# Crossbar transposes for half of the q and k of a sliding-window attention with an MLP behind it

## The chip, the cores and the metric

One core of a Trainium2 chip. The metric is device time in microseconds (us), median of several executions; lower is better. Names used below: TensorE (matmuls and their weight loads, PE and PEld in the profile), VectorE (DVE), ScalarE (ACT), GpSimd (POOL), SyncE (SP, which here issues nearly all DMAs). SBUF and PSUM are the two memories that these kernels use: their tiles lie in SBUF, TensorE's results in PSUM. A "hole" is a stretch in which TensorE is idle. Ratios are always the mean time of one kernel's fast runs over the mean of the other's fast runs of the same rounds, so they are not quite the ratio of the medians quoted. A run counts as slow when it is over 1.5% above the fastest run of the same kernel.

## The reference

Attention with a causal window of 64 over 8 batches, 8 heads, 576 tokens, head dimension 64; then, per token, a normalisation and a two-layer MLP of 512 to 2048 to 512 with ReLU, added to the attention's output.

```python
scores = scale * np.matmul(q, k.transpose(0, 1, 3, 2))
mask = (rel >= 0) & (rel < 64)             # rel = query position - key position
attn = softmax(np.where(mask, scores, -1e9))
x = np.matmul(attn, v)                      # heads side by side: (8, 576, 512)
xn = (x - mean) / np.sqrt(var + 1e-6) * g_ln
out = x + np.maximum(xn @ w_ch1, 0.0) @ w_ch2
```

## The kernel before

The kernel works in nine groups. Group g runs the MLP of batch g on the first 512 tokens; group 8 runs it for the last 64 tokens of all batches, which were collected as four "tails" of two batches each. From group 2 on, the MLP of group g is cut into 30 units (16 of the first layer, 14 of the second, which is done with seven products instead of eight). Work for other batches is placed between the units, at numbered slots: the attention of batch g+1, and the loads, casts and transposes of batch g+2. So a slot is a place in the program order of every engine.

The kernel transposes q and k for the scores, so that the head dimension lies on the partitions. Before, TensorE does it, 128x128 at a time, and ScalarE moves the result out of PSUM:

```python
def t_main(b, x, half, eng=None):               # x: 0 for q, 1 for k
    tp = t_tile([128, 8, 128], ...)
    for i in range(8):
        nc.tensor.transpose(out=tp[:, i, :], in_=src[:, i], identity=ident16)
    ...
    evac(x if eng is None else eng, dst..., tp...)

def cast_tail(i):                               # GpSimd, in this order
    vt = p_va.tile([128, 2, H, D + 1], FP16, tag="vt", bufs=1)
    nc.gpsimd.memset(vt[:, :, :, D:D + 1], 1.0)
    nc.gpsimd.tensor_copy(out=q16, in_=tq)
    nc.gpsimd.tensor_copy(out=k16, in_=tk)
    nc.gpsimd.tensor_copy(out=vt[:, :, :, 0:D], in_=tv)

# the schedule of groups 2 to 7; n = g + 2
at(11, cast_qk, n, 0)
at(16, cast_qk, n, 1)
for i, (x, half) in zip((17, 19, 21, 25), ((0, 0), (1, 0), (0, 1), (1, 1))):
    at(i, t_main, n, x, half, 0)
at(27, s_mm, n, 0)                              # first scores of batch n
at(17, load_qk, n + 1, 0)                       # 1 MB each
at(18, load_qk, n + 1, 1)
at(23, load_v, n + 1, 0, 4)
# tails: loads at slot 5, cast at 24, transposes at 27 and 29, scores at slot 1 of the next group
# stores of the group's own rows stand in units 27 and 29
```

The softmax here doesn't subtract the row's maximum and nothing guards it: scores larger than these inputs give would overflow.

## Time and profile before

| | before |
|---|---|
| median of 2 runs | 324.47 us (324.37 to 324.57) |
| span in the profile | 322.6 us |
| TensorE busy | 309.6 us, 96% |
| mean granted clock | 0.996 |
| idle TensorE up to its last matmul, summed from the matmul records | 7.6 us, of it 1.4 us after 90 us |

The first lines are from the page of the kernel before: the busy row of TensorE, the clock granted to TensorE in 40 slices (tenths of full speed), and the main DMA queue (packets, MB, share of 16 engines' time).

```profile
PE 309.6 (96%) x3229; PEld 204.6 (63%) x3229; DVE 204.3 (63%) x388; ACT 176.8 (55%) x292; POOL 164.6 (51%) x251
...
PEclk9999999999999999999999999999999999999998
...
q1 hardware_dynamic: 84816, 48.11, 55.6%
```

The next lines are from the chain of waits of the kernel before (start, length, what), in the second half of group 3. They follow each other without a hole: TensorE is always the one waited for. The pieces "tp x8" are eight transposes of q or k, 0.45 us together, 56 ns each (the first piece of a group, shown here, stands in the chain with 0.55 us). (The group table gives 225 ns for one; as eight take 0.45 us together, they overlap.)

```profile
149.72 1.75 PE pA L435 x16
151.47 0.38 PE xps L291 x16
151.85 0.55 PE tp L216 x8
152.40 0.87 PE pB L435 x8
...
162.92 0.34 PE sc L263 x16
163.26 1.85 PE pC L435 x16
```

And SyncE's own timeline of the kernel before for the same group (start, time at the instruction, operation). The loads of the next batch's first half are at 147.8 us, those of the second half at 153 us. v follows at 158.8 and the stores at 163.7 us.

```profile
147.81 0.39 SPq L92 DMA_DIRECT2D qk<-in_q_dram  x1
148.80 0.39 SPq L92 DMA_DIRECT2D qk<-in_k_dram  x1
152.95 0.37 SPq L92 DMA_DIRECT2D qk<-in_q_dram  x1
153.94 0.37 SPq L92 DMA_DIRECT2D qk<-in_k_dram  x1
158.82 4.68 SPq L139 DMA_DIRECT2D v<-in_v_dram  x4
163.68 4.14 SPq L401 DMA_DIRECT2D out_dram<-xn  x4
```

### The profile page before, as it was taken

To read this page: it belongs to the slowest core of one execution; us is meant where nothing else is said; L and a number is where in the kernel's file an instruction comes from. 1 tells how busy PE (TensorE), PEld (TensorE's weight loads), DVE (VectorE), ACT (ScalarE), POOL (GpSimd) and SP (SyncE) were. 2 spreads that over 40 slices of the span, in tenths; PEclk is the share of its full clock that TensorE was granted. 3 is DMA by queue.
4 is the path that set the end of the run, shared out by engine and by line. 5 is a ranking of instruction groups with operands and counts; after the bars stand their busy time and mean duration, and the time that the engine had idled before them with its cause. 6 is when DMAs were issued, how large, how long until landed. Compare 5 with 4: busy or idle time off the path is not lost.

```text
span 322.6 us, 7813 instructions
## 1 busy us (share of the span) xinstructions
PE 309.6 (96%) x3229; PEld 204.6 (63%) x3229; DVE 204.3 (63%) x388; ACT 176.8 (55%) x292; POOL 164.6 (51%) x251
## 2 busy tenths in 40 slices
PE   7978999999989999999999999999999999999993
PEld 4556444687544578656964696459755865694582
DVE  0887764666885795489447954896559644751643
ACT  2576624487346754876457647775486157405600
POOL 7678765423991689079705982598036506200000
PEclk9999999999999999999999999999999999999998
DMA  8999999976089947904598459000570190003013
GB/s 194 282 385 259 363 306 295 264 267 133 35 276 227 207 139 204 241 2 133 173 259 183 132 168 259 26 2 2 171 182 2 24 241 33 0 2 131 0 36 98
DMA packets 85639, 51.08 MB, mean 158 GB/s; under 512 B 55682, under 2 KB 76674, under 8 KB 85603
## 3 DMA queue, kind: packets, MB, share of 16 engines
q1 hardware_dynamic: 84816, 48.11, 55.6%
q0 software_dynamic: 640, 2.33, 3.1%
q8 instruction: 25, 0.41, 0.5%
q10 hardware_dynamic: 146, 0.13, 0.1%
q14 instruction: 12, 0.09, 0.1%
HBM read 38.80 MB, written 9.44 MB: 150 GB/s over the span
## 4 chain that ended last, share of the span: by engine, by line
PE 85%; DVE 4%; SPq 3%; DMA 2%; POOL 2%; ACT 1%; issue 0%; ACTq 0%; POOLq 0%
PE hps L363 33%; PE pA L435 11%; PE pC L435 8%; PE pB L435 8%; PE hph L484 6%; PE ch L375 4%; PE xps L291 4%; PE tp L216 3%; PE sc L263 3%; DMA w1s<-in_moe_w_ch_dram 2%; PE ztp L328 2%; SPq L139 2%; POOL w1g L188 1%; PE ch L499 1%; DVE wT L532 1%; SPq L87 1%
## 5 line engine op out<-in xcount | busy, mean ns | idle before, releaser
L363 PE MATMUL hps<-zT,w1g 128*128 128x512 f16 x480 | 112.0, 379 | 0.0
L367 ACT ACTIVATE hrT<-hps 128x512 f16<-128x512 f32 x120 | 71.9, 599 | 35.1 <-PE hps L363 31.6
L363 PEld LDWEIGHTS <-w1g 128*128 128x128 f16 x480 | 44.1, 98 | 47.0 <-issue 1.0
L316 POOL TENSOR_SCALAR rsz<-mvg 128x1 f32<-128x1 f32 x28 | 12.2, 437 | 76.5 <-DVE mvg L302 75.5
L266 ACT ACTIVATE pt<-sc 128x512 f16<-128x512 f32 x72 | 39.0, 595 | 14.6 <-PE sc L263 13.1
L435 PEld LDWEIGHTS <-sS 128*128 128x128 f16 x448 | 43.0, 98 | 4.7
L207 ACT COPY qkT<-tp 128x1024 f16<-128x1024 f16 x26 | 26.2, 1012 | 33.6 <-PE tp L216 32.4
L126 POOL CAST qk<-qk 128x1024 f16<-128x1024 f32 x32 | 33.7, 1070 | 9.5 <-DMA qk<-in_q_dram 4.9
L442 DVE TENSOR_TENSOR xn<-pA,xn 128x512 f32<-128x512 f32 x28 | 19.2, 686 | 26.1 <-PE pA L435 17.4
L331 ACT COPY zT<-ztp 128x512 f16<-128x512 f16 x36 | 21.1, 586 | 26.5 <-PE ztp L328 26.1
L435 PEld LDWEIGHTS <-hrT 128*128 128x128 f16 x336 | 32.3, 98 | 5.0
L294 DVE RECIPROCAL rcp<-xps 128x8 f32<-128x8 f32 x36 | 7.4, 205 | 34.3 <-PE xps L291 34.1
L414 DVE TENSOR_TENSOR sS<-hrT 128x512 f16<-128x512 f16 (+1 forms) x42 | 21.4, 510 | 10.2 <-ACT hrT L367 10.2
L297 DVE TENSOR_TENSOR xn<-xps,rcp 128x512 f32<-128x512 f32 x36 | 24.9, 692 | 3.3 <-DMA out_dram<-xn 2.2
L435 PE MATMUL pA<-wT,sS 128*128 128x256 f16 x224 | 26.9, 273 | 0.0
L435 PE MATMUL pC<-w2s,sS 128*128 128x256 f16 x224 | 26.8, 273 | 0.0
L273 DVE TENSOR_TENSOR pt<-pt,mask 128x1024 f16<-128x1024 f16 x28 | 21.2, 762 | 8.6 <-ACT pt L266 8.5
L484 PE MATMUL hph<-zT,w1g 128*128 128x256 f16 x192 | 23.6, 273 | 2.5 <-ACT zT L331 1.1
L299 DVE BATCH_NORM_STATS2 stats<-xn 128x6 f32<-128x512 f32 x36 | 25.0, 695 | 1.2
L319 POOL TENSOR_SCALAR z<-xn,rsz 128x512 f16<-128x512 f32 x28 | 23.4, 836 | 2.9
L375 PE MATMUL ch<-w2s,hrT 128*128 128x512 f16 x96 | 23.7, 380 | 0.1
L484 PEld LDWEIGHTS <-w1g 128*128 128x128 f16 x192 | 18.0, 98 | 5.8 <-issue 2.2
(85 smaller groups left out, 437.2 us busy)
## 6 DMA issues: line engine op xcount, KB each, us to landing
out_dram<-xn SPq DMA_DIRECT2D x34, 256.0 KB, 3.6
qk<-in_q_dram SPq DMA_DIRECT2D x16, 512.0 KB, 4.8
qk<-in_k_dram SPq DMA_DIRECT2D x16, 512.0 KB, 5.9
v<-in_v_dram SPq DMA_DIRECT2D x32, 256.0 KB, 6.2
w2s<-in_moe_w_ch_dram SPq DMA_DIRECT2D x12, 512.0 KB, 5.6
w1s<-in_moe_w_ch_dram SPq DMA_DIRECT2D x4, 512.0 KB, 7.3
tk<-in_k_dram SPq DMA_DIRECT2D x8, 256.0 KB, 4.4
tv<-in_v_dram SPq DMA_DIRECT2D x8, 256.0 KB, 5.1
```

The costliest lines, as they stand in the source:

```text
L126: nc.gpsimd.tensor_copy(out=dst[:, :].rearrange("p (a j) e d -> p a e j d", j=j), in_=t[:, :].rearrange("p (a e j d) -> p a e j d", e=2, j ...
L207: nc.scalar.copy(out=out, in_=in_)
L266: nc.scalar.activation(out=pt[:, par], in_=sc[par], func=AF.Exp, bias=0.0, scale=scale)
L297: nc.vector.tensor_tensor(out=xn, in0=xps[:, :, 0:D], in1=rcp_b, op=ALU.mult)
L299: nc.vector.bn_stats(out=stats, in_=xv)
L319: nc.gpsimd.tensor_scalar(out=z, in0=xv, scalar1=rs, scalar2=nm, op0=ALU.mult, op1=ALU.add)
L363: nc.tensor.matmul(out=hps, lhsT=w1g[:, kc, 128 * hc:128 * (hc + 1)], rhs=zT[g][:, kc, :], start=(kc == 0), stop=(kc == NKC - 1),)
L367: nc.scalar.activation(out=hrT[:, hc, :], in_=hps, func=AF.Relu, bias=0.0, scale=1.0)
L375: nc.tensor.matmul(out=ch[kb], lhsT=hrT[:, hc, 128 * kb:128 * (kb + 1)], rhs=w2s[:, hc, :], start=(hc == 0), stop=(hc == NHC - 1),)
L414: nc.vector.tensor_tensor(out=o, in0=x, in1=y, op=op)
L435: nc.tensor.matmul(out=bank[which][:, p, :], lhsT=a[:, c, 128 * p:128 * p + 128], rhs=wv[:, c, :], start=(first and p == 0 and c == 0), st ...
L484: nc.tensor.matmul(out=hps[:, e], lhsT=w1g[:, kc, 128 * hc:128 * (hc + 1)], rhs=zT[g][:, kc, 256 * half:256 * half + 256], start=(kc == 0) ...
```

## The change

Intent: take the transposes of q and k of batches 4 to 7, and of all tails, off TensorE and let the DMA crossbar do them, from SBUF to SBUF. The casts now write to two fixed buffers, of which the tails share k's (not shown in the cut below). The transposed layout differs, so k is loaded in its natural order (runs of 256 bytes), q stays in an order of four interleaved tokens, and the exponential puts it right by its access pattern. v loads move behind the stores; the residual buffers of groups 4 and later swap places, so that the next group's first block takes the one that was stored first.

```diff
+    XQ = 4
+            elif b >= XQ and x == 1:            # load_qk: k in natural order
+                for c in range(2):
+                    nc.sync.dma_start(out=..., in_=src[b, :, s0:s0 + 128, :].rearrange("h s d -> s h d"))
 def t_main(b, x, half, eng=None):
+        if b >= XQ:
+            if half == 0:
+                nc.sync.dma_start_transpose(out=dst..., in_=cast16[x]...)      # 512 KB
+            return
 # t_tail: the same, dma_start_transpose for q and for k of a tail
-            nc.scalar.activation(out=pt[:, par], in_=sc[par], func=AF.Exp, ...)
+            if XQ <= g < NGRP - 1:
+                o = o.rearrange("p h w (r j) -> p (h w) r j", j=4)
+                i = i.rearrange("p h w (j r) -> p (h w) r j", j=4)
+            nc.scalar.activation(out=o, in_=i, func=AF.Exp, ...)
+                for h in ((1, 0) if g // 2 == 2 else (0, 1)):                   # b_step: pairs swap homes
+                    x_norm[(g, h)] = p_xn.tile(...)
-            ts = (10, 11, 14, 20) if n else (1, 2, 5, 11)
+            ts = (10, 11, 15, 20) if n else (5, 6, 10, 15)
-            for i, ... in zip((17, 19, 21, 25), ...
+            for i, ... in zip((17, 17, 17, 17) if n >= XQ else (17, 19, 21, 25), ...
-                at(23, load_v, n + 1, 0, 4)
+                at(31, load_v, n + 1, 0, 4)
-                at(24, cast_tail, i)
-                at(27, t_tail, i, 0)
-                at(29, t_tail, i, 1)
+                at(22, cast_tail, i)
+                at(22, t_tail, i, 0)
+                at(22, t_tail, i, 1)
```

More of the change, by code (lines that the diff above doesn't have):

```diff
@@ L41 @@
     EPS = 1e-6
+    XQ = 4
+    XZ = 99
     scale = 1.0 / (D ** 0.5)
@@ L77 @@
     qk32, qk16, v32 = {}, {}, {}
+    cast16 = [p_const.tile([128, NHP, 4, 128], FP16, tag=f"cast16_{x}", name=f"cast16_{x}") for x in range(2)]
     tail32, tail16, tailT, vT = {}, {}, {}, {}
@@ L90, in load_qk @@
                 )
+            elif b >= XQ and x == 1:
+                for c in range(2):
+                    s0 = 256 * half + 128 * c
+                    nc.sync.dma_start(
+                        out=t[:, 512 * c:512 * c + 512].rearrange("p (h d) -> p h d", h=H),
+                        in_=src[b, :, s0:s0 + 128, :].rearrange("h s d -> s h d"),
+                    )
             else:
@@ L110, in cast_tail @@
         q16 = p_in.tile([128, H, D], FP16, tag="tq16", name=f"tq16_{i}", bufs=1)
-        k16 = p_in.tile([128, 2, H, D], FP16, tag="qk16_1", name=f"tk16_{i}")
+        k16 = cast16[1][:, 0:2].rearrange("p r c (e d) -> p r (c e) d", d=D)
         vt = p_va.tile([128, 2, H, D + 1], FP16, tag="vt", name=f"vt_{i}", bufs=1)
@@ L122, in cast_qk @@
             t = qk32.pop((b, x, half))
-            dst = p_in.tile([128, 8, 2, D], FP16, tag=f"qk16_{x}", name=f"qk16_{x}_{b}_{half}")
+            if b >= XQ and x == 1:
+                nc.gpsimd.tensor_copy(
+                    out=cast16[x][:, :, 2 * half:2 * half + 2, :].rearrange("p a c m -> p c a m"),
+                    in_=t[:, :].rearrange("p (c a m) -> p c a m", c=2, a=NHP),
+                )
+                continue
+            dst = cast16[x][:, 2 * half:2 * half + 2, :, :].rearrange("p a c (e d) -> p (a c) e d", d=D)
             qk16[(b, x, half)] = dst
@@ L202, in alloc_qkT, with flat @@
         qkT[b] = [p_qkt.tile([128, NHP, SM + 64 * x], FP16, tag=f"qkT{x}", name=f"qkT{x}_{b}") for x in range(2)]
-        nc.gpsimd.memset(qkT[b][1][:, :, 0:64], 0.0)
+        if b < XQ:
+            nc.gpsimd.memset(qkT[b][1][:, :, 0:64], 0.0)
+        else:
+            nc.gpsimd.memset(qkT[b][1][:, 0, 0:64], 0.0)
+    def flat(b, x):
+        return qkT[b][x][:, :, :].rearrange("p h m -> p (h m)")
     def evac(x, out, in_):
@@ L211, in t_main @@
     def t_main(b, x, half, eng=None):
+        if b >= XQ:
+            if half == 0:
+                dst = flat(b, x)[:, 64 * x:64 * x + NHP * SM]
+                nc.sync.dma_start_transpose(out=dst.rearrange("p (a t) -> p a t", t=128),
+                                            in_=cast16[x][:, :, :, :].rearrange("p a c m -> p (a c m)"))
+            return
         src = qk16.pop((b, x, half))
@@ L229, in t_tail @@
                         p_qkt.tile([128, 2, NHP, 128], FP16, tag="tkT", name=f"tkT_{i}", bufs=1))
+            if XQ < B:
+                nc.sync.dma_start_transpose(out=tailT[i][0], in_=src[:, :, :].rearrange("p h d -> p (h d)"))
+                return
             tp = t_tile([128, NHP, 128], f"tpq_{i}")
@@ L233, in t_tail @@
         else:
+            if XQ < B:
+                nc.sync.dma_start_transpose(out=tailT[i][1][:, :, :, :].rearrange("p r h t -> p (r h) t"),
+                                            in_=src[:, :, :, :].rearrange("p r h d -> p (r h d)"))
+                return
             tp = t_tile([128, 2, NHP, 128], f"tpk_{i}")
@@ L258, in s_mm @@
                         rhs = tailT[j][0][rows, hp, 64 * iw:64 * iw + 64]
+                    elif g >= XQ:
+                        c0 = SM * hp + 64 * (2 * j + iw)
+                        lhsT = flat(g, 1)[rows, c0:c0 + 128]
+                        qb = flat(g, 0)[rows, SM * hp + 16 * (2 * j + iw):SM * hp + 16 * (2 * j + iw) + 16]
+                        rhs = bass.AP(tensor=qb.tensor, offset=qb.offset, ap=[qb.ap[0], [128, 4], [1, 16]])
                     else:
@@ L265, in s_mm @@
         for par in range(2):
-            nc.scalar.activation(out=pt[:, par], in_=sc[par], func=AF.Exp, bias=0.0, scale=scale)
+            o, i = pt[:, par], sc[par][:, :]
+            if XQ <= g < NGRP - 1:
+                o = o.rearrange("p h w (r j) -> p (h w) r j", j=4)
+                i = i.rearrange("p h w (j r) -> p (h w) r j", j=4)
+            nc.scalar.activation(out=o, in_=i, func=AF.Exp, bias=0.0, scale=scale)
     def s_mask(g, j):
@@ L278, in b_step @@
         if kb % 2 == 0:
-            x_norm[(g, kb // 2)] = p_xn.tile([128, 2, DM], FP32, tag="xn" + sfx, name=f"xn_{g}_{kb // 2}", bufs=nb)
+            if (g, kb // 2) not in x_norm:
+                for h in ((1, 0) if g // 2 == 2 else (0, 1)):
+                    x_norm[(g, h)] = p_xn.tile([128, 2, DM], FP32, tag="xn" + sfx, name=f"xn_{g}_{h}", bufs=nb)
         xv = x_norm[(g, kb // 2)][:, kb % 2, :]
@@ L325, in zt_step @@
             zT[g] = p_grp.tile([128, NKC, 512], FP16, tag="zT" + sfx, name=f"zT_{g}", bufs=1 if sfx else 2)
+        if g >= XZ:
+            nc.sync.dma_start_transpose(out=zT[g][:, :, 128 * kb:128 * kb + 128], in_=z)
+            return
         ztp = t_tile([128, NKC, 128], f"ztp_{g}_{kb}")
@@ L745 @@
             at(21, make_vB, n)
-            for i, (x, half) in zip((17, 19, 21, 25), ((0, 0), (1, 0), (0, 1), (1, 1))):
+            for i, (x, half) in zip((17, 17, 17, 17) if n >= XQ else (17, 19, 21, 25),
+                                    ((0, 0), (1, 0), (0, 1), (1, 1))):
                 at(i, t_main, n, x, half, 0)
```

## The prediction

> **What bounds the kernel now.** TensorE. It is busy for 96% of the 322.6 us span (engine table; granted clock 0.996), and the chain of waits is 85% TensorE. From about 98 us to 317 us that chain is an almost unbroken row of matmul pieces. So in groups 2 to 8 a TensorE instruction removed should shorten the run by its own pace, and a new TensorE wait should lengthen it in full.
>
> **Removed from TensorE.** The instruction order shows 352 fewer load and matmul rows: 176 transposes, 32 in each of batches 4 to 7 (128) and 12 in each of four tails (48). The chain shows eight of them as pieces of 0.45 us (56 ns each; the 225 ns mean of one is latency). 22 pieces x 0.45 = 9.9 us. All lie on the chain. ScalarE also loses 16 evacuations of 1.01 us and eight for tails, off the chain. Without new waits: 324.5 - 9.9 = 314.6 us.
>
> **Added.** Sixteen crossbar transfers on the SyncE queue: per batch q and k, 512 KB each, plus two smaller ones per tail. [...] No trace shows one yet. Batch k loads now come in 256-byte runs, as v does. Exponentials now read PSUM strided; I expect the same 595 ns.
>
> **Main batches.** In the timeline of group 3 the last q/k cast ends at 153.9 us and the first scores of that batch start at 162.85 us. Taking out 1.8 us of transposes leaves about 7.1 us for both transfers. [...] on time, or late by up to 1 or 2 us, four times. Expected cost 1 us in all, with a long tail. v loads now follow the stores, and swapping residual pairs gives a group's first attention block the buffer stored first (2.2 us of VectorE wait before, off the chain).
>
> **A new wait in group 7.** The fourth tail's cast starts with a memset of the single buffered v tile, so GpSimd waits until TensorE has used the third tail's (before: 10.8 us of GpSimd wait, hidden). That use moves from slot 5 to slot 10, and the fourth tail's scores stay in slot 10, directly behind it in TensorE's order. Between them must now fit: memset 0.15, q cast 0.6, k cast 1.0 (durations in the timeline at 268 us), the crossbar transfer of k and its landing [...]. TensorE stops for about 5 us. This gives back half of the gain.
>
> **Prediction.** 314.6 + 5 + 1 = about 320.5 us, range 315 to 327. Faster by over 2%: 0.27; within 2%: 0.65; slower: 0.08.
>
> **What would show it.** TensorE busy falls by about 10 us by pace; groups 3 to 6 last 1.5 to 2 us less each (now 32 to 33.5 us); one TensorE wait of 4 to 6 us at the scores of the fourth tail, on a DMA; at the first scores of batches 4 to 7 waits on the crossbar transfers of 0 to 2 us; exponentials near 595 ns.
>
> **What would make it wrong.** Crossbar transfers much slower (q and k over 8 us together): TensorE waits four times, and the run is slower than before. Much faster ones: the group 7 wait shrinks to 3 us and the change gains over 2%. Scores reading q in 16-element runs being slower.

The sum came to 314.6 + 5 + 1 = 320.6, put as about 320.5 us, with 314.6 = 324.5 - 9.9. The 5 and the 1 are estimates.

## The result, and the profile after

347.75 us, median of 2 runs (347.25 to 348.24); ratio 1.0717, 95% interval 1.065 to 1.0785. The change makes the kernel 7% slower.

The same rows of the page, after:

```profile
PE 310.0 (89%) x3053; PEld 197.6 (57%) x3053; DVE 207.9 (60%) x388; ACT 156.0 (45%) x268; POOL 162.6 (47%) x251
...
PEclk9999999999999999699996999899999999899999
...
q1 hardware_dynamic: 120272, 53.88, 66.1%
```

TensorE is busy for as long as before, although it executes 176 matmuls less (3053 instead of 3229), and the clock row now has four dents. The time between the starts of the groups' first layers says where it was lost:

| group | 2 | 3 | 4 | 5 | 6 | 7 |
|---|---|---|---|---|---|---|
| before, us | 32.8 | 33.3 | 32.8 | 33.3 | 30.6 | 29.2 |
| after, us | 30.9 | 40.0 | 38.0 | 41.1 | 29.9 | 35.3 |

Groups 2 and 6 are faster, as intended. TensorE's matmul records show one long hole in each of the others: 3.3 us at 137 us (before the first tail's scores), 4.3 us at 179 us (before an attention block), 5.2 us at 215 us (before the second tail's scores), 5.4 us at 290 us (before the fourth tail's). The waits view of the kernel after (who waits for whom: us in total, times, longest) names the releasers, first for TensorE, then for VectorE:

```profile
PE sc L303 <- DMA tkT<-cast: 13.9, 3, 5.4
PE xps L337 <- DVE pt L317: 5.0, 2, 4.3
...
PE sc L303 <- DMA qkT<-cast: 0.9, 2, 0.5
```

```profile
DVE xn L343 <- DMA out_dram<-xn: 23.5, 3, 9.4
```

Before, VectorE's line for the same wait was:

```profile
DVE xn L297 <- DMA out_dram<-xn: 2.2, 3, 1.7
```

So stores of the residual buffers free these too late, by up to 9.4 us; VectorE then gives the attention block's masks late (before the hole at 179 us ends, its L343 starts at 180.92 us after 6.59 us of idle, the mask behind it at 182.47 us), and TensorE waits for VectorE ("pt L317"). The transposed q and k of the main batches, by contrast, cost 0.9 us in two waits: they are not the problem. Here is SyncE's timeline after, from the end of group 2 into group 3:

```profile
119.90 5.09 SPq L237 DMA_TRANSPOSE qkT<-cast  x2
125.04 0.59 SPq L102 DMA_DIRECT2D qk<-in_q_dram  x1
125.67 2.34 SPq L97 DMA_DIRECT2D qk<-in_k_dram  x2
128.06 1.54 SPq L102 DMA_DIRECT2D qk<-in_q_dram  x1
129.64 4.39 SPq L97 DMA_DIRECT2D qk<-in_k_dram  x2
134.13 2.74 SPq L259 DMA_TRANSPOSE tqT<-tq  x1
136.96 1.25 SPq L266 DMA_TRANSPOSE tkT<-cast  x1
138.31 2.00 SPq L450 DMA_DIRECT2D out_dram<-xn  x4
```

Two transposes hold the queue for 5.1 us. Then all six loads of the next batch, 2 MB, are issued together, for 9.0 us (DMA share 1.1 from 125 to 134 us, 1.2 to 140 us); before, half of them had gone at slot 17, ahead of this place, because their buffers were free. Only then come the tail's transposes (134 us) and the stores (138 us), one after the other.

What a hole does to the clock is seen in the windows view of the kernel after. Columns: the stretch, its length, busy us (and instructions) of PE, PEld, DVE, ACT, POOL, the granted clock, the DMA share, GB/s. The hole before the first tail's scores ends at 140.1 us; from 141.45 to 148.3 us the clock is halved.

```profile
139.00:141.00 2.00, 0.91 (x19) 0.60 (x20) 0.00 (x0) 0.47 (x1) 0.00 (x0) 1.00 1.07 352
141.00:143.00 2.00, 2.00 (x7) 0.49 (x4) 1.46 (x3) 1.11 (x3) 0.00 (x0) 0.61 0.99 257
143.00:145.00 2.00, 1.32 (x34) 1.10 (x34) 1.81 (x5) 0.63 (x2) 1.61 (x3) 0.50 1.04 234
145.00:147.00 2.00, 2.00 (x9) 0.89 (x8) 1.93 (x5) 1.26 (x3) 1.37 (x3) 0.50 0.90 198
147.00:149.00 2.00, 2.00 (x9) 0.80 (x8) 1.18 (x2) 1.17 (x3) 1.77 (x3) 0.68 0.31 69
```

The trace's clock record has four such stretches, of 6.8, 6.8, 3.4 and 3.4 us; leaving out the parts in which TensorE was idle anyway, about 18.5 us. From one 128x512 matmul of the first layer to the next it is 0.427 us at half clock (145 to 148 us) and 0.216 us at full clock, so half of that time is lost: 9.3 us. In the kernel after, full and half clock take turns from 11.75 us on, for 129.71, 6.83, 34.13, 6.83, 30.72, 3.41, 71.68, 3.41 and 47.79 us, all whole multiples of 3.41 us. When the trace is cut into pieces of that length, from 11.75 us on, the four at whose end the clock fell held 2.05, 3.41, 3.35 and 3.41 us of idle TensorE; none of the others held more than 1.84 us. The first of the four ends at 141.45 us, with 2.05 us of the 3.3 us hole in it. In the kernel before, whose longest hole is 1.4 us, the clock did not fall before the last matmul. What a piece with 1.84 to 2.05 us of idle does, these two traces do not show.

This closes the account of the time: 9.9 us of transposes less, 23.5 us of idle TensorE more (31.0 against 7.6), 9.3 us lost at half clock: +22.9 us, against a measured 346.5 - 322.6 = 23.9 us of span.

Two things that the change could have spoilt, it did not: the exponentials take 595 ns with the reordering pattern as without, and sixteen score matmuls take 0.34 us in the chain as before.

### The profile page after: what moved, and what is told of

The parts are those of the page before. It is cut to its first block, busy times and chain, and to the rows that moved or that the text cites. A ratio compares the mean times of both kernels' runs of the same rounds, so it can differ in the third digit from the quotient of the medians.

```text
span 346.5 us, 7472 instructions
## 1 busy us (share of the span) xinstructions
PE 310.0 (89%) x3053; PEld 197.6 (57%) x3053; DVE 207.9 (60%) x388; ACT 156.0 (45%) x268; POOL 162.6 (47%) x251
## 4 chain that ended last, share of the span: by engine, by line
PE 57%; POOL 10%; SPq 9%; DVE 8%; DMA 7%; ACT 4%; issue 3%; POOLq 0%; DVEq 0%; ACTq 0%
PE hps L412 23%; PE hph L533 6%; PE pA L484 6%; PE pC L484 4%; PE pB L484 4%; SPq L97 3%; PE xps L337 3%; PE ch L424 3%; DMA out_dram<-xn 3%; PE sc L303 2%; SPq L102 2%; DMA vB<-vA 2%; ACT pt L310 2%; DVE stats L345 2%; DVE xn L343 2%
## 5 line engine op out<-in xcount | busy, mean ns | idle before, releaser
L412 PE MATMUL hps<-zT,w1g 128*128 128x512 f16 x480 | 118.0, 397 | 0.0
L412 PEld LDWEIGHTS <-w1g 128*128 128x128 f16 x480 | 46.1, 101 | 53.0 <-issue 8.8
L343 DVE TENSOR_TENSOR xn<-xps,rcp 128x512 f32<-128x512 f32 x36 | 24.9, 691 | 24.6 <-DMA out_dram<-xn 23.5
L491 DVE TENSOR_TENSOR xn<-pA,xn 128x512 f32<-128x512 f32 x28 | 19.2, 685 | 21.6 <-PE pA L484 16.6
L463 DVE TENSOR_TENSOR sS<-hrT 128x512 f16<-128x512 f16 (+1 forms) x42 | 23.8, 566 | 10.1 <-ACT hrT L416 10.1
L317 DVE TENSOR_TENSOR pt<-pt,mask 128x1024 f16<-128x1024 f16 x28 | 21.8, 785 | 12.6 <-ACT pt L310 12.6
L142 POOL CAST cast<-qk 128x1024 f16<-128x1024 f32 x24 | 25.3, 1061 | 8.4 <-DMA qk<-in_q_dram 3.9
L337 PEld LDWEIGHTS <-pt 128*64 128x64 f16 x576 | 12.5, 113 | 19.1 <-issue 8.2
L363 POOL TENSOR_TENSOR rsz<-rsz,mhalf 128x1 f32<-128x1 f32 x28 | 20.2, 721 | 2.3
```

Source lines behind the costliest of these rows:

```text
L142: nc.gpsimd.tensor_copy(out=dst[:, :].rearrange("p (a j) e d -> p a e j d", j=j), in_=t[:, :].rearrange("p (a e j d) -> p a e j d", e=2, j ...
L337: nc.tensor.matmul(out=xps[64 * r:64 * r + 64, h, :D + 1], lhsT=pt[:, par, hp, r, :], rhs=rhs, start=True, stop=True)
L343: nc.vector.tensor_tensor(out=xn, in0=xps[:, :, 0:D], in1=rcp_b, op=ALU.mult)
L412: nc.tensor.matmul(out=hps, lhsT=w1g[:, kc, 128 * hc:128 * (hc + 1)], rhs=zT[g][:, kc, :], start=(kc == 0), stop=(kc == NKC - 1),)
L463: nc.vector.tensor_tensor(out=o, in0=x, in1=y, op=op)
```

## The experiments

Eighteen kernels were run in all, in five sessions, each with its own runs of before. "Idle" is idle TensorE up to its last matmul in the profiled run.

| run | what | median us | ratio to before | 95% interval | idle us |
|---|---|---|---|---|---|
| before | | 324.5 to 325.2 by session | | | 7.6 |
| after | | 347.75 | 1.072 | 1.065 to 1.079 | 31.0 |
| e1 | q and k on the crossbar, tails on TensorE | 337.24 | 1.039 | 1.034 to 1.045 | 21.4 |
| e2 | q and k loads behind the stores | 328.40 | 1.010 | 1.005 to 1.015 | 17.9 |
| e3 | memset of the v tile after the casts | 340.95 | 1.047 | 1.042 to 1.053 | 24.7 |
| e4 | stores issued by GpSimd | 347.19 | 1.069 | 1.063 to 1.076 | 30.6 |
| e5 | k in 1 KB runs (order of keys wrong) | 340.76 | 1.049 | 1.046 to 1.051 | 27.9 |
| e6 | tails alone on the crossbar | 331.53 | 1.020 | 1.018 to 1.023 | 14.5 |
| e7 | first half of q, k loaded early | 333.74 | 1.028 | 1.025 to 1.031 | 22.1 |
| e8 | e2 with idle matmuls in the hole of group 7 | 328.87 | 1.008 | 1.004 to 1.013 | 16.3 (slow run) |
| s1 | v loads and swapped pairs alone | 324.32 | 0.999 | 0.997 to 1.000 | 7.4 |
| b1 | e2 and e3 together | 325.40 | 1.001 | 0.999 to 1.002 | 16.2 |
| b3 | b1, first half loaded early | 327.18 | 1.009 | 1.005 to 1.013 | 15.5 |
| b4 | b1, two steps in later slots | 325.26 | 1.001 | 0.997 to 1.004 | 14.2 |
| f1 | e6 with idle matmuls in the hole of group 7 | 329.62 | 1.015 | 1.012 to 1.018 | 10.1 |
| b5 | b1, tails of groups 3 and 5 moved to group 6 | 327.27 | 1.007 | 1.005 to 1.010 | 17.6 |
| b6 | b5 with later slots | 326.33 | 1.004 | 1.002 to 1.006 | 17.1 |
| b7 | b1 with k in 1 KB runs (order of keys wrong) | 320.81 | 0.987 | 0.984 to 0.989 | 12.5 |
| b9 | b6, tail transposes and loads behind the stores | 325.67 | 1.002 | 1.000 to 1.004 | 16.6 |
| b10 | b9 with only batches 6 and 7 on the crossbar | 331.66 | 1.018 | 1.016 to 1.021 | 19.5 (slow run) |

The first theory was a queue theory: SyncE's order holds tail transposes and stores behind the loads. Its rival was traffic: crossbar reads and short runs fill the DMA engines, whatever the order.

### e1: tails back on TensorE

```diff
-            if XQ < B:                     # t_tail, twice
+            if XT:                         # XT = False
-            ts = (10, 11, 15, 20) if n else (5, 6, 10, 15)
+            ts = (10, 11, 14, 20) if n else (1, 2, 5, 11)
-                at(22, cast_tail, i); at(22, t_tail, i, 0); at(22, t_tail, i, 1)
+                at(24, cast_tail, i); at(27, t_tail, i, 0); at(29, t_tail, i, 1)
```

> The changed kernel with the tails' transposes back on TensorE, in the slots of before; q and k of batches 4 to 7 stay on the crossbar. Queue theory (one in-order SyncE queue holds tail transposes and stores behind six loads; TensorE then idles 3.3, 4.3, 5.2 and 5.4 us and its clock halves after each): the three waits for the tails' transposed k go (13.9 us, and about 7 us of their half clock), 48 transposes come back (2.7 us): about 330 us, and the 4.3 us gap at 179 us, which is a late store, stays. Traffic rival (crossbar reads and 256-byte k loads fill the DMA engines, so every transfer is late whatever the order): the tails' waits go but VectorE waits for stores as long as before (over 20 us), about 337 to 343 us.

337.2 us: between the two. The holes for transposed tails are gone, but others of 3.9, 2.7, 1.8 and 5.3 us stand at the same three group starts (the one of 2.7 us waits for another DMA, a copy of v), and VectorE still waits 14.3 us for stores. The stores are now issued directly behind the six loads (at 133.5, 170.8 and 204.4 us), and still too late. So the tail transposes were not what held the stores. In front of them are left the two transposes and the six loads; e2 tells which. This also prices the main half of the change: q and k alone on the crossbar cost 12 us over the 325.2 us of before.

### e2: q and k loads behind the stores

```diff
-                at(17, load_qk, n + 1, 0)
-                at(18, load_qk, n + 1, 1)
+                at(31, load_qk, n + 1, 0)
+                at(31, load_qk, n + 1, 1)
```

> The changed kernel with the q and k loads of the next batch moved from directly behind the transposes to behind the stores; nothing else. Same bytes, same packets. Queue theory: tail transposes and stores are issued about 9 us earlier, the gaps at 137, 179 and 215 us (3.3, 4.3, 5.2 us) and their half clock go, the one in group 7 stays: 326 to 330 us; the casts of q and k may now wait for their loads by some us. Traffic rival: the traffic is the same, so about 345 to 348 us with the gaps somewhere else.

328.4 us, as the queue theory said: 19 us from two lines, with the same bytes in the same packets. The stretch of SyncE's timeline of e2 that answers to the one shown above:

```profile
120.25 5.04 SPq L237 DMA_TRANSPOSE qkT<-cast  x2
128.25 1.26 SPq L259 DMA_TRANSPOSE tqT<-tq  x1
129.96 1.23 SPq L266 DMA_TRANSPOSE tkT<-cast  x1
131.28 2.00 SPq L450 DMA_DIRECT2D out_dram<-xn  x4
133.34 0.75 SPq L102 DMA_DIRECT2D qk<-in_q_dram  x1
```

The stores are issued at 131.3 instead of 138.3 us, and the three holes at 137, 179 and 215 us are gone; of VectorE's 23.5 us of waits for stores 0.6 us are left. What remains of TensorE's waits is group 7's and small ones:

```profile
DVE xn L343 <- DMA out_dram<-xn: 0.6, 1, 0.6
```

```profile
PE sc L303 <- DMA tkT<-cast: 5.4, 1, 5.4
PE ztp L377 <- POOL z L365: 4.2, 3, 1.4
...
PE sc L303 <- DMA qkT<-cast: 1.9, 3, 0.8
```

### e3: one memset later

```diff
-        nc.gpsimd.memset(vt[:, :, :, D:D + 1], 1.0)
         nc.gpsimd.tensor_copy(out=q16, in_=tq)
         nc.gpsimd.tensor_copy(out=k16, in_=tk)
+        nc.gpsimd.memset(vt[:, :, :, D:D + 1], 1.0)
```

> The changed kernel with one line moved: in the cast of a tail the memset of the v tile comes after the casts of q and k, not before. It tests the wait in group 7 alone: the fourth tail's k is cast and transposed long before its scores. Theory of the prediction: the 5.4 us gap at 290 us and the 3.4 us at half clock behind it go, 347.7 - 5.4 - 1.7 = about 340.6 us, all else as it was. Rival, that the crossbar transfer itself is slow there: the gap stays, 347 us.

340.95 us, 0.3 us from the number expected. First the kernel after, GpSimd's timeline in group 7: the memset waits for TensorE's third tail (14.48 us of idle GpSimd), and the casts come behind it, right when TensorE wants the fourth tail's scores.

```profile
290.30 0.17 POOL L125 MEMSET vt<- 128x16 f16 x1 [14.48 <-PE xps L337]
...
290.98 1.04 POOL L127 CAST cast<-tk 128x1024 f16<-128x1024 f32 x1
```

In e3 both casts run before the memset, which now waits alone, and the hole of 5.4 us is gone:

```profile
280.13 1.04 POOL L126 CAST cast<-tk 128x1024 f16<-128x1024 f32 x1 [0.32 <-DMA tk<-in_k_dram]
286.19 0.17 POOL L127 MEMSET vt<- 128x16 f16 x1 [5.01 <-PE xps L337]
```

### e4: stores on another queue

```diff
-            nc.sync.dma_start(out=out[g, ...], in_=x_norm[...])
+            (nc.gpsimd if g > 1 else nc.sync).dma_start(out=out[g, ...], in_=x_norm[...])
```

> The changed kernel with the stores of groups 2 to 7 issued by GpSimd instead of SyncE. Queue theory: the stores start when VectorE has finished them, VectorE's 23.5 us of waits for stores fall under 5 us, the 4.3 us gap at 179 us goes; the tails' transposes are still behind the loads, so the gaps of 3.3, 5.2 and 5.4 us stay: 337 to 341 us. Traffic rival: stores land as late as before, VectorE's waits stay over 15 us, 345 to 348 us.

347.2 us: no gain, the expectation missed. GpSimd does issue the stores early, at 129.8 and 131.3 us (SyncE: 138.3 us), but they land late: a median of 6.6 us after their issue, against 3.5 us for the stores of the kernel after, and VectorE still waits 14 us for them. The issuing engine alone does not explain this: in e4 the twelve stores beside the bursts of groups 2 to 4 took 6.0 to 8.4 us, the four of group 7, with little else under way, 2.4 to 4.7 us. The lines are from e4's list of DMA issues and from its waits view:

```profile
out_dram<-xn POOLq DMA_DIRECT2D x24, 256.0 KB, 6.6
```

```profile
DVE xn L343 <- DMA out_dram<-xn: 14.0, 4, 4.7
```

So a free queue was not enough here (347.2 us against 347.75). The waits for transposed tails, which still stand behind the loads, even grew from 13.9 to 17.4 us.

Both pure theories had failed: the queue alone (e1, e4) and the traffic alone (e2, where the traffic is the same). What fits all four runs is a burst theory: the 2 MB of loads, issued in one piece behind the transposes, occupy the DMA engines for about 9 us, and whatever is issued after them, on any queue, is late. The order decides what is in front. The next runs test that.

### e5: longer runs for k

```diff
-            elif b >= XQ and x == 1:
+            elif False:                    # k goes the way of q, in 1 KB runs
```

> The changed kernel with k of batches 4 to 7 loaded in runs of 1 KB as before instead of 256 bytes (the order of tokens is then wrong and so is the result, on purpose; the work is the same). Burst theory, as the first four runs left it: 2 MB of q and k loads are queued at once between the transposes and the stores and fill the DMA engines for about 9 us; the size of the runs only changes how long. The loads take 1 to 2 us less per batch, the gaps at 137, 179 and 215 us shrink but stay: 338 to 344 us. Rival, that the 256-byte runs are the cause: those three gaps go, 326 to 330 us.

340.8 us, inside the range of the burst theory: the holes shrink to 1.0 and 1.5, 1.5 and 2.5, and 3.3 us and stay. The keys are then in a wrong order. The comparison with the reference passed it all the same. A likely reason, only argued: q and k are 0.1 times standard normal numbers, the scaled scores then have a spread of about 0.01, and all weights in a window are nearly equal. It is no version to use; it also means that this comparison would hardly notice a permuted k, in any of the kernels.

### e6: tails alone

```diff
-    XQ = 4
+    XQ = 8
-            if XQ < B:                     # t_tail, twice
+            if True:
```

> One part of the change alone: tails on the crossbar, with their new slots, v loads behind the stores and the pairs swapped; q and k of all batches on TensorE as before, so that the q and k loads start early again. Burst theory: no gap at the starts of groups 3 to 5; the gap of 5.4 us in group 7 and its half clock (1.7 to 3.4 us) stay; 48 transposes less give 2.7 us: 325.2 - 2.7 + 7 to 9 = 329 to 331 us. Rival, that crossbar transfers delay the stores by themselves: gaps over 2 us at the starts of groups 3 and 5, 335 us or more.

331.5 us, 0.5 us above the range of the burst theory: no hole at any group start, only group 7's (5.4 us) and 6.8 us at half clock. By themselves the tails' transfers did not delay the stores here: e6's waits view has no wait of VectorE for a store (23.5 us in the kernel after).

### e7: half of the loads ahead of the transposes

```diff
-                at(17, load_qk, n + 1, 0)
+                at(13, load_qk, n + 1, 0)
```

> The changed kernel with the loads of the first half of q and k moved from slot 17, behind the two transposes in SyncE's order, to slot 13, ahead of them: their buffers are free from slot 12 on, as before the change. Burst theory: half of the 2 MB is through before the transposes start; what stands in front of the tail transposes and the stores halves, so the gaps at 137, 179 and 215 us fall from 3 to 5 us to under 2 us and most of their half clock goes: 328 to 335 us with group 7's gap left. Rival, that transposes and tails alone delay the stores: 343 us or more.

333.7 us. The holes fall to 0.6, 1.6 and 2.2 us; VectorE's wait for stores halves, from 23.5 to 12.0 us. With half of the burst in front of the stores, half of the wait is left.

### e8 and f1: what the clock costs

The 5.4 us hole of group 7 was filled with 20 matmuls of 128x512 into an unused bank, first in e2, then in e6.

```diff
+            if n:
+                at(ts[0], fill_clock, 20)   # before the fourth tail's scores
```

> The kernel with the q and k loads behind the stores (328.4 us; one gap of 5.4 us in group 7 and 6.9 us at half clock behind it), with 20 idle matmuls of 128x512 put into that gap, about 4.3 us of them at full clock, so that TensorE waits as long but is not idle. Theory: the half clock is a consequence of the idle gap and costs half of its length, 3.4 us: about 325 us. Rival, that the clock falls for another reason, or that its length in the record costs nothing: 328.4 us or more.

328.9 us: six runs spread from 324.75 to 331.3 us, two of them slow. The half clock of group 7 was gone from the profile, but that profile was of a slow run, and another hole, of 4.0 us at batch 6's transposed k, had come with a half clock of its own. e2's own four runs had spread over 3.4 us. So it was repeated in e6, whose runs lie within 1.3 us:

> The kernel with only the tails on the crossbar (331.5 us, its four runs within 1.3 us, one idle gap of 5.4 us in group 7 and 6.9 us at half clock behind it), with 20 idle matmuls of 128x512 in that gap. The gap is as long, but TensorE is busy in it. Theory: the half clock comes from the idle gap and costs half its length: 331.5 - 3.4 = about 328 us and no half clock in groups 7 and 8. Rival: the clock is not what costs, 331 us or more.

329.6 us, 1.9 us less than e6, and no half clock until the end. TensorE still had to wait as long: 4.3 us of filling (20 times 0.216 us, the pace of the 128x512 matmuls in the chain), and 0.9 us of waiting that is left, by the waits view of f1:

```profile
PE sc L303 <- DMA tkT<-cast: 0.9, 1, 0.9
```

So in these two runs it was the idle hole that brought the half clock (mean clock of the profiled runs 0.985 in e6, 0.999 in f1). The expected 3.4 us were too many: of the 6.8 us at half clock in e6 the first 2.8 fell into the hole itself (clock halved at 275.0, hole over at 277.8 us), and half of the other 4.1 us is 2.0, which is what was measured.

### s1: the rest of the change alone

```diff
# the kernel before, with
+                for h in ((1, 0) if g // 2 == 2 else (0, 1)): ...
-                at(23, load_v, n + 1, 0, 4)
+                at(31, load_v, n + 1, 0, 4)
```

> The other part of the change alone, on the kernel before: v loads behind the stores and the residual pairs swapped, no crossbar at all. Theory: these two cost nothing by themselves, TensorE has no wait in either kernel: within 1 us of before. Rival, that moving v behind the stores is what makes later transfers late: 3 us or more above before.

324.3 us, ratio 0.999: the order of v and the swapped pairs are harmless by themselves, and worth nothing measurable.

### b1, b3, b4: the repairs together

b1 is e2 plus e3. b3 loads the first half at slot 13 and only the second half behind the stores. b4 is b1 with

```diff
-            at(27, s_mm, n, 0); at(28, s_mask, n, 0)
+            at(29, s_mm, n, 0); at(30, s_mask, n, 0)
-                at((8, 13, 18, 23)[j], zt_step, b, j)
+                at((8, 13, 19, 23)[j], zt_step, b, j)
```

> Both repairs together: q and k loads behind the stores, and the memset of the v tile after the casts. Theory: the repairs add up, 328.4 - 5.4 - 1.7 to 3.4 = 320 to 322 us, 1 to 1.5% faster than before; TensorE's idle time after 100 us is under 6 us. Rival, that group 7's gap hides another wait behind it: 325 us or more.

> As the last, but the first half of q and k is loaded ahead of the transposes (slot 13) and only the second half behind the stores. Burst theory: nothing but the transposes stands in front of the stores, and the loads are spread over two quiet stretches, so the transposes of the next batch no longer meet late loads: 318 to 321 us. Rival: loads ahead of the transposes make these land later, waits of 1 us or more at the first scores of batches 4 to 7: 322 to 326 us.

> As the kernel with both repairs, with the first scores of the next batch two slots later (29 instead of 27) and the transposes of the third normalised block one slot later (19 instead of 18). Theory: the waits of 0.5 to 0.8 us for transposed q and k and of 1.4 us for the third block, two to four times each, go: 3 to 5 us less than the kernel with both repairs, 316 to 319 us. Rival: these waits are made up later anyway, same time.

325.4, 327.2 and 325.3 us: all three miss their ranges, and none beats before. b1's profile tells why; first its busy row, then its waits. TensorE is busy 8.6 us less than before (309.6), so the removed transposes do show; but it is idle 8.6 us more.

```profile
PE 300.9 (93%) x3053; PEld 194.3 (60%) x3053; DVE 204.8 (63%) x388; ACT 155.3 (48%) x268; POOL 162.7 (50%) x251
```

```profile
PE ztp L377 <- POOL z L365: 5.1, 4, 1.4
PE sc L303 <- DMA qkT<-cast: 4.0, 3, 3.1
```

The largest single wait is 3.1 us at the first scores of batch 6, for its transposed k. Its two transposes are issued at 184.6 us, when six tail loads, issued from 179 us on, have only just gone out; they occupy SyncE for 6.6 us and the DMA share is 1.3 there. The other additions are waits of 1.4 us for a normalised block; before, the transposes that stood between may have covered them, which is argued and not tested. In b4 each of two such waits splits into one of 0.5 and one of 0.7 us, the small waits for k are gone, and its profile still has a hole of 3.5 us at batch 6, with 6.8 us at half clock, which begin inside it. b1's profile flatters it: it is of its fastest run (324.3 us, clock 0.997), and the other four fast runs have a clock of 0.991 or 0.992, lower than any run of before (0.995). By these numbers some 3 us at half clock, an estimate, are missing from the profile; in it the hole at batch 6 (3.06 us of idle TensorE between 190 and 196 us) was not followed by half clock: the granted clock is 1.00 in every window from there to 199 us.

### b5, b6, b9, b10: making room

b5 moves the tails of groups 3 and 5 to group 6, so that no tail load meets the busy groups; b6 adds the later slots.

```diff
-    TAILS = {3: [0], 5: [1], 7: [2, 3]}
+    TAILS = {6: [0, 1], 7: [2, 3]}
-                at(5, load_tail, i)
+                at(12, load_tail, i)
-            at(7, t_tail, TAILS[g][1], 0); at(8, t_tail, TAILS[g][1], 1)
+            at(4, t_tail, TAILS[g][1], 0); at(4, t_tail, TAILS[g][1], 1)
```

> Both repairs (325.4 us), and the tails of groups 3 and 5 done in group 6, so that their loads fall into group 5, where the DMA engines have little else. Theory: what holds the kernel with both repairs at the time of before is the wait of 3 to 4 us for the transposes of batch 6, which meet the tail loads still in flight (DMA share over 1.3 at 184 to 190 us); it goes: 319 to 322 us. Rival: the crossbar transfers are slow beside any loads: still 3 us or more of waits at the first scores, 324 us or more.

> As the last, with the first scores of the next batch at slot 29 and the transposes of the third and fourth normalised block one or two slots later. Theory: the rest of the waits (0.4 to 0.6 us for transposed q and k, 1.4 us for normalised blocks) go as well, 3 us less than the last: 316 to 319 us, near 324.5 - 9.9 plus 1 to 3. Rival: no difference to the last.

327.3 and 326.3 us, both slower than b1. In b5 the wait at batch 6 did fall, from 3.1 to 0.5 us, so the tail loads had a part in it (b7, below, takes the hole away with the tail loads in place). But in group 5 the second tail's loads, at slot 25, now stood in front of the stores, and the mistake of the change was made again in small; VectorE's timeline of b6:

```profile
233.23 0.69 DVE L343 TENSOR_TENSOR xn<-xps,rcp 128x512 f32<-128x512 f32 x1 [8.54 <-DMA out_dram<-xn]
```

b9 puts these loads and the tail transposes behind the stores as well; b10 leaves batches 4 and 5 on TensorE (XQ = 6).

> As the kernel with the late tails and later slots (326.3 us), with the tail transposes and the second tail's loads behind the stores as well and the second tail's steps three slots later: nothing but the transposes of q and k is left in front of the stores. In the last kernel VectorE waited 8.5 us for a store that stood behind six tail loads. Theory: this wait goes, 5.9 us of idle TensorE and the half clock behind it: 318 to 321 us, 1 to 2% faster than before. Rival: the tail transposes now come too late for their scores, 323 us or more.

> The same with only batches 6 and 7 on the crossbar (batches 4 and 5 transposed by TensorE). 64 transposes more on TensorE cost 3.6 us; in exchange the DMA engines carry 2 MB less of transposes and k comes in long runs for two batches more. If the crossbar's traffic still costs TensorE waits in groups 2 and 3: same or faster than the other. If not: 3 to 4 us slower, 321 to 325 us.

b9: 325.7 us. The wait for stores is gone, but tails that are loaded and transposed later come too late for their scores in groups 6 and 7 (waits of 0.5, 1.0 and 3.0 us), and the attention block waits for VectorE twice (1.8 and 1.6 us). b10: 331.7 us, with a profile of a slow run; why it is 6 us above b9, when 64 transposes cost 3.6 us, was not settled. That profile has a hole of 4.3 us at batch 7's transposed k and one of 3.9 us at a tail's, with 10.2 us at half clock.

### b7: short runs in the repaired kernel

> Both repairs (325.4 us) with k loaded in runs of 1 KB again (wrong result on purpose). Tells whether the 256-byte runs are what keeps the DMA engines full when the tail loads and the transposes of batch 6 meet. If so, that wait falls from 3 us to under 1 us: 321 to 323 us. If the number of bytes is what counts: 325 us.

320.8 us, at the lower end of what was expected if the short runs matter: b1 with k in 1 KB runs (the edit of e5) is 4.6 us faster than b1 (ratios to before 0.987 and 1.001) and 1.3% faster than before. The hole at batch 6 is gone; of the waits for transposed q and k 1.1 us in two are left:

```profile
PE sc L303 <- DMA qkT<-cast: 1.1, 2, 0.6
```

The DMA packets of b1 take 236 us (summed, over 16 engines), those of b7 225 us, those of before 192 us. So in the repaired kernel it is the natural-order load of k, which this change's transposed layout asks for, that gives back the gain. It is the only run that clearly beats before, and its keys are in the wrong order; no correct version that beats before was found.

## Why the prediction was wrong

- **What bounds the kernel, and the 9.9 us.** Right. Group 2 became 1.9 us shorter (32.8 to 30.9), and b1's TensorE is busy 8.6 us less.
- **The transposes of the main batches, "on time, or late by up to 1 or 2 us, four times; expected cost 1 us".** Right: two waits, 0.9 us together. In the first of the four batches it took 119.9 to 128.4 us from the issue of the first transfer to the landing of the second, 8.5 us for 1.05 MB, or 123 GB/s with the latency in it; in the others 6.8 to 8.0 us. From 121 to 125 us, before the loads were issued, the DMA engines moved 200 GB/s. The slots left room for what was measured.
- **The new wait in group 7, "TensorE stops for about 5 us".** Right: 5.4 us, and e3 removes it by the memset that was named. Missing was the clock: half speed behind it, 1.5 us more in the kernel after, 2 us in e6.
- **"v loads now follow the stores, and swapping residual pairs gives a group's first attention block the buffer stored first."** This is the step that failed, together with the "two smaller ones per tail", which got no wait except in group 7. It was read as protecting the stores, and VectorE's 2.2 us of waits for them as off the chain. Measured, these waits became 23.5 us and reached TensorE (5.0 us at "pt L317"), and the transposed k of the first and the second tail came 3.3 and 5.2 us too late. I had looked at what moved behind the stores and not at what was now in front of them. Before, half of the next batch's loads went out ahead of the transposes' slot; after, the two waiting crossbar transfers held SyncE, and all 2 MB followed in one burst of 9.0 us, in front of tail transposes and stores. e2 moves the loads and recovers 19 us, s1 shows that v and the pairs were not the cause, and e4 shows that a second queue did not help once the burst was out (347.2 us).
- **No term for the clock.** The sum had one pure wait of 5 us. In fact holes of 3.3 to 5.4 us came with 18.5 us of work at half clock: 9.3 us, a term nearly as large as the whole gain.
- **"What would make it wrong"** named slow crossbar transfers or slow scores. The scores and exponentials did not slow down. The pairs of transfers took 6.8 to 8.5 us, around the 8 us that were named, and still cost TensorE only 0.9 us. The loss came from transfers that the change did not touch, only pushed together.
- **Short runs.** "Batch k loads now come in 256-byte runs, as v does" was noted and given no cost. In the kernel after it is 7 us (e5 against after), and in the repaired kernel 4.6 us (b7 against b1).

## What to carry to other kernels

When work moves to DMAs, write down the issuing queue's whole order, before and after, and ask of each urgent transfer (a store that frees a buffer, a transfer that the next matmul needs) what now stands in front of it, in the queue and in the engines; a transfer that waits for data early in the order can turn what stands behind it into a burst (here 2 MB of loads, issued in 9.0 us behind two transposes). Put what frees buffers in front of what fills them for later. And where TensorE is the bound, count a hole twice: once as the wait, and again for the work at half clock that can follow it (in the kernel after, each of the holes of 3.3 to 5.4 us was followed by 3.4 or 6.8 us at half clock, those of up to 1.4 us by none; in b1 one of 3.06 us by none).

## What was measured of the crossbar, the transposes and the stores

- Crossbar: two transfers of 512 KB, SBUF to SBUF, took 6.8 to 8.5 us from the issue of the first to the landing of the second in the kernel after, 123 to 154 GB/s with the latency in it; from 121 to 125 us, before the loads were issued, the engines moved 200 GB/s. The median from issue to landing of one is 5.1 us (4.3 to 7.0), against 6.1 us for a q load of 512 KB in the same run.
- What it costs the issuing engine: 4.1 to 5.7 us of SyncE for two in the kernel after, against 0.37 to 0.39 us for a q or k load of 512 KB in the kernel before (from 114 us on).
- TensorE: in the chain of the kernel before, eight transposes of 128x128 in a row cost 0.45 us, 56 ns each. A decision made with the 225 ns that the group table gives for one would be four times too hopeful.
- Stores: in the kernel after, issued in order on SyncE, the median from issue to landing is 3.5 us; issued by GpSimd beside the bursts (e4, groups 2 to 4) they took 6.0 to 8.4 us.
